# A list scheduler whose order comes from one rule, and then from three tables of offsets, leads and margins

## The chip, the cores and the metric

The kernel runs on one NeuronCore of a Trainium2 chip. The metric is the device time of one execution in microseconds (us), lower is better. Engines: PE (TensorE), DVE (VectorE), ACT (ScalarE), POOL (GpSimd) and SP (SyncE, which here issues nearly all DMAs).

## The reference: what is computed

Sliding-window attention, then a 2-D Fourier mixing, a layer norm, and a two-layer feed-forward network, all with residuals:

```python
# q, k, v: (8, 8, 576, 64); window 64
scores = np.where(mask, scale * q @ k.T, -1e9); attn = softmax(scores)
x = (attn @ v)                                   # -> (8, 576, 512)
u = x + np.real(np.fft.fft(np.fft.fft(x, axis=1), axis=2))
un = (u - mean) / sqrt(var + 1e-6)
out = u + np.maximum(un @ w_ch1, 0) @ w_ch2      # w_ch1 (512, 2048), w_ch2 (2048, 512)
```

The weights arrive as 64-bit floats, q, k and v as 32-bit floats.

## The kernel before

The 4608 rows are 36 tiles T of 128 rows (9 tiles for each pair of batches) and 18 chunks c of 256 rows for the feed-forward part. Five families of steps are declared and handed to one list scheduler:

- `attn_tile(T)`: loads kn, qn, v (L433), brings keys and queries into place (tiles below 13, the "whole" ones, by PE transposes pk, pq; the later, "split" ones as pairs of 16-bit halves, by DMA transposes, L493, L505), scores psc (L574, L581), masked maximum (L593, DVE), exponential (L601, ACT), the transposed probabilities pt (PE transpose pp, or halves `p_hi`, `p_lo` in the buffer flex and DMA transposes L632), the product pa (L663), its scaling xu (L670, L673, L682 or L680), a first radix-4 step y (L704) and its transpose py (by PE, L769 and L773, or by halves yp, L409 or L411 and L781, and a DMA transpose, L788).
- `fft(b)`, one for each batch: folds and radix steps on DVE and POOL (L815 to L850), halves fs and hs (L869), PE stages pg (L901) and pz (L933), and the results md, sent to DRAM (L961).
- `norm_tile(T)`: a gather mt from DRAM (L1011), the statistics and un (L1023 to L1039), its halves up (`u_hi` L409 or L413, `u_lo` L1058) and a DMA transpose into uhl (L1063); the first chunk uses PE transposes pu (L1051).
- `weight_piece`, `weight_scale`, `weight_split`: 32 loads of 512 KB (L1103; tiles wd or flex), three DVE conversions each (L1112, L1117, L1124), squares on ACT (L1130), a scale from the sum of squares (few L1167, the PE product pw L1148, L1151 and on), halves (L409 and L1177).
- `ffn(c)`: 16 steps f; ph (12 matmuls of 256 columns, L1220), relu hh on ACT (L1235) and its lower half on DVE (L1238), po (6 matmuls of 512 columns, L1201).

`Plan.order` simulates the five engines and picks, again and again, the step that can start first. Ties and small differences go by `prio` (`base` plus a constant written at each call); a step that may run on either of two engines takes the other one if that is sooner by more than `margin`. Buffers are rings of few slots (`RINGS`): kq 2, up 1, pt 2, big 4, ps 4 banks; for most rings the slots are handed out in the order of `prio`. Each engine then executes its list strictly as it was emitted, so an instruction that waits holds back all behind it on its engine. The ring up has one slot: the halves of a normed tile (`up`) or of a radix-4 result (`yp`) may be written only after the DMA transpose of the tile before them has landed.

In the start phase, where the planner finds PE idle for over 0.8 us, the kernel inserts small dummy matmuls (warm, L1300; called fillers here).

Of the kernel before, what the change touches and what calls it, by code (L numbers as in the profile page):

```python
# [127 lines left out]


class Op:  # L130
    __slots__ = ("eng", "dur", "lat", "fn", "deps", "outs", "prio", "wait", "ready", "allocs", "bufs", "idx", "durs", "margin", "port", "slack", "wary")


class Plan:
# [13 lines left out]
    def __init__(self, rings, fifo):  # L148
        self.rings, self.fifo, self.ops, self.gaps = dict(rings), fifo, [], []
        self.slack = self.wary = 0.0  # L150

    def op(self, eng, dur, prio, fn, reads=(), writes=(), lat=0.0, alt=(), holds=(), port=True):

        o = Op()
        o.durs = {e: d + self.FIXED[e] for e, d in ([(eng, dur), alt[:2]] if alt else [(eng, dur)])}
        o.port, o.slack, o.wary = port, self.slack, self.wary
        o.margin = alt[2] if len(alt) > 2 else self.MARGIN
        o.eng, o.dur, o.lat, o.fn, o.prio = eng, dur, lat, fn, prio  # L160
        o.idx, o.outs, o.allocs = len(self.ops), [], []
        deps = set()
        for b in reads:
            deps.update(b.writers)
        for b in writes:
            deps.update(b.writers)
            deps.update(b.readers)
            if b.ring and not b.writers and b not in o.allocs:
                o.allocs.append(b)
# [132 lines left out]
def attn_fft_ffn_kernel(ctx: ExitStack, tc: tile.TileContext, q, k, v, w1, w2, gidx, dft_d, dft_s, mask, out):  # L302
# [14 lines left out]
    plan = Plan(RINGS, ("kq", "pr", "pt", "xu", "y", "yT", "tail", "xe", "r3", "fh", "g", "mp", "f1", "f2", "hh"))  # L317
# [99 lines left out]
    def attn_tile(T, base):  # L417
# [145 lines left out]
        for jj in range(2):  # L563
# [42 lines left out]
            if whole:  # L606

                def flip_p(jj=jj):
# [7 lines left out]
                   alt=("DVE", 0.6), port=False)  # L616
# [93 lines left out]
        for bb in range(2):  # L710
# [3 lines left out]
            b = b0 + bb  # L714
# [284 lines left out]
    def norm_tile(T, base):  # L999
# [88 lines left out]
    def weight_piece(x, g, order):  # L1088
# [243 lines left out]
```

## Time and profile before

| | us |
|---|---|
| median of 3 runs | 1012.32 (1011.74 to 1016.52) |
| span of the profiled execution, first to last instruction | 1008.1 |
| median less span | 4.2 |
| PE busy | 973.4 (97%) |
| PE weight load busy | 694.3 (69%) |
| DVE busy | 682.6 (68%) |
| ACT busy | 445.8 (44%) |
| POOL busy | 155.1 (15%) |

The profiled execution's own total is not given apart from its span; what lies around the span is taken as the 4.2 us to the median. A matmul's record includes its fill, so PE counts as busy for a little of the time in which it waits; the distance from one step's start to the next is the better measure of its pace.

### The profile page before, as it was taken

The numbers are of one execution on the slowest core, as the hardware profiler recorded it, in microseconds if no ns is written. First come the engines' busy times: TensorE is split into PE (matmuls) and PEld (weight loads), VectorE is DVE, ScalarE is ACT, GpSimd is POOL, SyncE is SP. The second block draws the span as 40 slices with busy tenths as digits, with TensorE's granted clock in tenths as the row PEclk, the third lists the DMA queues.
The fourth block names the chain that finished last, engine by engine and source line by source line (L and its number), as shares of the span: only waits on it lengthen the run. The fifth ranks groups of instructions, "written<-read, shape, count | busy, mean of one in ns | idle before, by whom it ended". The sixth has DMA issues, their size and how long they took to land.

```text
span 1008.1 us, 22813 instructions
## 1 busy us (share of the span) xinstructions
PE 973.4 (97%) x8831; PEld 694.3 (69%) x8831; DVE 682.6 (68%) x1979; ACT 445.8 (44%) x1257; POOL 155.1 (15%) x162
## 2 busy tenths in 40 slices
PE   8897999999999999989999999999999999999998
PEld 6886767766676667666676666666676667666664
DVE  4699998788696779776787558776786645442121
ACT  6788756653554345443444445433443223121111
POOL 1000102011212221231023322031011100200000
PEclk9999999999999999999999999999999999999999
DMA  9999875334975796778767865968554311230000
GB/s 208 224 230 228 215 185 150 74 64 94 159 157 124 147 157 116 146 148 142 143 118 167 156 123 87 180 142 152 100 111 100 84 33 45 53 74 22 1 21 21
DMA packets 310955, 123.60 MB, mean 123 GB/s; under 512 B 292728, under 2 KB 292856, under 8 KB 310848
## 3 DMA queue, kind: packets, MB, share of 16 engines
q1 hardware_dynamic: 308128, 113.24, 56.2%
q0 software_dynamic: 2720, 8.92, 3.3%
q8 instruction: 69, 1.13, 0.5%
q14 instruction: 38, 0.31, 0.1%
HBM read 54.97 MB, written 14.17 MB: 69 GB/s over the span
## 4 chain that ended last, share of the span: by engine, by line
PE 70%; DVE 10%; DMA 10%; SPq 3%; issue 3%; ACT 2%; POOL 1%; DVEq 0%; ACTq 0%; POOLq 0%
PE ph L1220 30%; PE po L1201 28%; PE pa L663 3%; DMA uhl<-up 2%; PE pz L933 2%; DMA mt<-md,gix 2%; PE psc L581 2%; PE psc L574 1%; PE pg L901 1%; DVE y L704 1%; SPq L632 1%; DMA wd<-in_moe_w_ch 1%; DVE hh L1238 1%; PE py L769 1%; DMA flex<-in_moe_w_ch 1%
## 5 line engine op out<-in xcount | busy, mean ns | idle before, releaser
L1220 PE MATMUL ph<-uhl,w0s 128*128 128x256 f16 (+1 forms) x3384 | 425.1, 276 | 12.1 <-DVE hh L1238 11.4
L1201 PE MATMUL po<-w1s,hh 128*128 128x512 f16 (+1 forms) x1696 | 425.9, 387 | 0.0
L1220 PEld LDWEIGHTS <-w0s 128*128 128x128 f16 x3264 | 317.4, 98 | 98.1 <-issue 16.1
L1235 ACT ACTIVATE hh<-ph 128x256 f16<-128x256 f32 x272 | 104.3, 383 | 397.7 <-PE ph L1220 283.7
L1238 DVE SCALAR_TENSOR_TENSOR hh<-ph,hh 128x256 f16<-128x256 f32 x272 | 114.6, 422 | 228.0 <-ACT hh L1235 207.7
L1201 PEld LDWEIGHTS <-hh 128*128 128x128 f16 x1632 | 156.3, 98 | 137.6
L601 ACT ACTIVATE pr<-pr,nm 128x128 f32<-128x128 f32 x288 | 90.8, 402 | 5.6 <-DVE nm L593 5.6
L593 DVE CUSTOM_DVE_ANT_0 pr<-psc,mskb 128x128 f32<-128x128 f32 x288 | 65.1, 285 | 16.0 <-PE psc L574 10.5
L680 ACT ACTIVATE xu<-pa,rc 128x64 f32<-128x64 f32 x248 | 54.9, 326 | 28.0 <-DVE rc L670 11.3
L1011 POOL DMA_INDIRECT mt<-md,gix x34 | 36.1, 1061 | 135.1 <-DMA md<-mp 129.8
L1035 POOL TENSOR_TENSOR rs<-mv,mhalf 128x1 f32<-128x1 f32 x36 | 20.8, 578 | 231.5 <-DVE mv L1031 224.7
L626 POOL TENSOR_TENSOR flex<-pr,flex 128x512 f16<-128x512 f32 x22 | 28.6, 1305 | 105.5 <-ACT flex L409 57.1
L663 PE MATMUL pa<-va,pt 128*64 128x65 f16 (+1 forms) x760 | 39.0, 204 | 1.6 <-DMA pt<-flex 1.2
L663 PE MATMUL pa<-ve,pt 128*64 128x65 f16 (+1 forms) x760 | 40.3, 205 | 0.0
L933 PE MATMUL pz<-g,ds__76 97*96 97x257 f16 (+3 forms) x240 | 29.7, 273 | 2.0 <-DVE g L911 2.0
L933 PEld LDWEIGHTS <-ds__76 97*96 97x96 f16 (+1 forms) x240 | 26.7, 124 | 4.2 <-issue 3.0
L501 POOL TENSOR_TENSOR flex<-qn,flex 128x1024 f16<-128x1024 f32 x11 | 23.7, 2159 | 37.5 <-ACT flex L409 28.7
L574 PE MATMUL psc<-kst,qbd 128*128 128x128 f32 x208 | 27.4, 281 | 1.6 <-ACT qbd L409 1.6
L663 PEld LDWEIGHTS <-pt 128*64 128x64 f16 x1104 | 20.0, 111 | 11.7 <-issue 9.9
L581 PEld LDWEIGHTS <-qbd 128*64 128x64 f16 x736 | 21.6, 110 | 8.4 <-issue 7.5
L704 DVE TENSOR_TENSOR y<-xu 128x256 f32<-128x256 f32 x64 | 25.6, 442 | 2.5 <-ACT xu L680 2.4
L574 PEld LDWEIGHTS psc<-kst,qbd 128*128 128x128 f32 x208 | 24.8, 192 | 3.5 <-issue 1.6
(160 smaller groups left out, 1120.9 us busy)
## 6 DMA issues: line engine op xcount, KB each, us to landing
wd<-in_moe_w_ch SPq DMA_DIRECT2D x20, 512.0 KB
out<-xu SPq DMA_DIRECT2D x36, 256.0 KB
ve<-va SPq DMA_DIRECT2D x67, 130.0 KB
kn<-in_k SPq DMA_DIRECT2D x32, 256.0 KB
qn<-in_q SPq DMA_DIRECT2D x32, 256.0 KB
flex<-in_moe_w_ch SPq DMA_DIRECT2D x12, 512.0 KB
flex<-in_v SPq DMA_DIRECT2D x20, 256.0 KB
md<-mp SPq DMA_DIRECT2D x24, 192.0 KB
```

Source lines behind the costliest of these rows:

```text
L574: nc.tensor.matmul(p_[:, hp], qw, keys(hp, jj), start=True, stop=True)
L581: nc.tensor.matmul(p_[64 * x : 64 * x + 64, hp], qbd[i][:, jj, h, 64 * z : 64 * z + 64], keys(h, jj), start=(z == 0), stop=(z == 1),)
L593: nc.vector.tensor_tensor_reduce(out=t["pr", jj][:, hp], in0=t["ps", jj][:, hp], in1=mskb[:, m : m + P], scale=-0.125, scalar=3.0e38, op0= ...
L601: nc.scalar.activation(pr, pr, AF.Exp, bias=t["nm", jj][:, hp : hp + 1], scale=-1.0)
L663: nc.tensor.matmul(pa[64 * jj : 64 * jj + 64, hh], pt[:, sl], v_, start=(x == 0), stop=(x == len(mm) - 1))
L680: nc.scalar.mul(xv[:, hh], pa[:, hh, 0:64], rc[:, hh])
L933: nc.tensor.matmul(pz[:M, c0:c1], ds_[:NJ, a, c[0] : c[0] + c[1]], t["g", gi][:, b_, c0:c1], start=(x == 0), stop=(x == len(mm) - 1),)
L1011: nc.gpsimd.indirect_dma_start(out=mts[T], out_offset=None, in_=mds[pb][0 : HR if n < 4 else 2 * HR], in_offset=bass.IndirectOffsetOnAxis( ...
L1201: nc.tensor.matmul(t["po"][i], l_, r_, start=(f == 0 and x == 0), stop=(f == NKF - 1 and x == len(mm) - 1))
L1220: nc.tensor.matmul(ph, l_, r_, start=(x == 0), stop=(x == len(mm) - 1))
L1235: nc.scalar.activation(t["hh", f][:, 0], ph, AF.Relu)
L1238: nc.vector.scalar_tensor_tensor(out=hh[:, 1], in0=ph, scalar=0.0, in1=hh[:, 0], op0=ALU.max, op1=ALU.subtract)
```

## The change

Nothing of the computation changes, nor the number of steps. Three tables come in, looked up by the kind of the group a step belongs to (`plan.begin(kind, at)`, called at the head of each attention tile, fft, norm tile, weight piece, scale and split) and by its place k in the group or by the group's number `at`. `NUDGE[kind][k]` and `LEAD[kind][at]` are added to the step's `prio`; `BIAS[kind][k]` is added to the margin of steps with two engines (20 keeps the first engine, -20 takes the other).

```diff
+NUDGE = {
...
+    "whole": (
+        -5.3, -1, 3.7, 0, 14.6, -3.5, 1.7, 3.6, -8.3, 1, 0.1, 0, 0, -1.4, 0.2, 1.9,
...
+LEAD = {
...
+    "whole": (
+        -54.4, -12, 0.6, 0, 0.5, -15.9, -4.6, -0.6, -4.3, 0, 9.1, 1.8, 0, -0.5, 0, -3.4,
...
+BIAS = {
...
+    "split": {16: 20, 19: 0.4, 23: -0.8, 26: -0.4, 29: -1.5, 31: 0.8, 33: -0.8, 34: 0.4, 35: 1.5, 36: -0.4, 37: 0.8},
...
+    def begin(self, kind, at):
+        self.kind, self.at, self.k = kind, at, 0
 
     def op(self, eng, dur, prio, fn, reads=(), writes=(), lat=0.0, alt=(), holds=(), port=True):
...
+        shift, lead = NUDGE.get(self.kind, ()), LEAD.get({"split": "whole", "odd": "even"}.get(self.kind, self.kind), ())
+        prio += (shift[self.k] if self.k < len(shift) else 0.0) + (lead[self.at] if self.at < len(lead) else 0.0)
...
+        bias = BIAS.get(self.kind, {}).get(self.k, 0.0)
+        self.k += 1
...
-        o.margin = alt[2] if len(alt) > 2 else self.MARGIN
+        o.margin = (alt[2] if len(alt) > 2 else self.MARGIN) + bias
...
+        plan.begin("whole" if whole else "split", T)
...
+        plan.begin("even" if bb == 0 else "odd", b)
...
+        plan.begin("norm", T)
...
+        plan.begin("piece", order)
...
+        plan.begin("scale", x)
...
+        plan.begin("part", W_ORDER.index((x, g)))
...
+        plan.begin("ffn", c)
```

The program has the same matmuls but for the fillers, 87 before and 81 now. DVE has 17 instructions fewer and ACT 22 more: the upper half of yp, which DVE made for ten of the 17 tiles that have one, is now always made by ACT. In the three places below, lines of the changed kernel count about 80 higher than those of the kernel before (L1103 is now L1183).

SP's queue in the start phase, from the loads of tile 4 on (ds is the second Fourier table, flex the weight pieces that are converted next). Before:

```order
L374 DMA ds__76<-in_dft_s 128x1924
L554 DMA ve0_83<-va1_82 64x520
L433 DMA va0_81<-in_v 64x8x64 x2
L1103 DMA flex_79<-in_moe_w_ch2 128x1024
L433 DMA kn5_569<-in_k 128x8x64
L546 DMA ve0_83<-va0_81 64x520
L433 DMA qn5_593<-in_q 128x8x64
L1103 DMA flex_79<-in_moe_w_ch2 128x1024
```

And now:

```order
L633 DMA ve0_83<-va1_82 64x520
L512 DMA va0_81<-in_v 64x8x64 x2
L1183 DMA flex_79<-in_moe_w_ch2 128x1024
L512 DMA kn5_564<-in_k 128x8x64
L625 DMA ve0_83<-va0_81 64x520
L452 DMA ds__76<-in_dft_s 128x1924
L1183 DMA flex_79<-in_moe_w_ch2 128x1024
L633 DMA ve1_84<-va0_81 64x520
L512 DMA qn5_647<-in_q 128x8x64
```

The table ds stands behind the first weight piece now, and qn5 behind the second one. Further down the same queue, kn8 stood behind va1 and now stands ahead of it.

DVE's queue at the scale of the first weight matrix (few0 is its sum of squares, the three w1s rows convert one weight piece, L593 and L672 are the masked maximum of tile 10). Before:

```order
L911 SCALAR_TENSOR_TENSOR g1_1_2001<-pg1_1_2000,g1_1_2001 97x512
L1112 TENSOR_SCALAR w1s_86<-wd1_12_1996 128x512
L1117 SCALAR_TENSOR_TENSOR w1s_86<-wd1_12_1996,w1s_86 128x512
L1124 SCALAR_TENSOR_TENSOR w1s_86<-wd1_12_1996,w1s_86 128x512
L1167 TENSOR_REDUCE few0_92<-ssq1_87 128x1
L593 ISA pr10_1_1763,nm10_1_2079<-psc10_1_1764,mskb_72 128x128
L593 ISA nm10_1_2079 128x1
```

And now:

```order
L672 ISA pr10_1_1845,nm10_1_2038<-psc10_1_1846,mskb_72 128x128
L672 ISA nm10_1_2038 128x1
L948 TENSOR_TENSOR hs0_1_2007<-h0_1_1916,hs0_1_2007 128x388
L1249 TENSOR_REDUCE few0_92<-ssq1_87 128x1
L1192 TENSOR_SCALAR w1s_86<-wd1_12_1990 128x512
L1197 SCALAR_TENSOR_TENSOR w1s_86<-wd1_12_1990,w1s_86 128x512
L1204 SCALAR_TENSOR_TENSOR w1s_86<-wd1_12_1990,w1s_86 128x512
L1232 TENSOR_SCALAR few0_92<-pw0_2062 128x1
L990 SCALAR_TENSOR_TENSOR g1_1_2013<-pg1_1_2012,g1_1_2013 97x512
```

The sum of squares and the masked maximum went ahead of the conversion, and g1_1 went behind it.

ACT's queue in chunk 4, around two users of the ring up (up11 and yp16; hh rows mark the steps of the feed-forward part). Before:

```order
L409 CAST up11_4633<-un11_4630 128x512
L1235 ACTIVATE hh4_4_4661<-ph4_4_4617 128x256
L534 ACTIVATE va0_81<-flex_79 128x8x64
L680 ACTIVATE xu16_4635<-pa16_0_4636,rc16_0_4674 128x64 x4
L680 ACTIVATE xu16_4635<-pa16_1_4540,rc16_1_4614 128x64 x4
L1235 ACTIVATE hh4_5_4712<-ph4_4_4617 128x256
L409 ACTIVATE yp16_4735<-y16_4714 128x512
L1235 ACTIVATE hh4_6_4744<-ph4_6_4719 128x256
```

And now (up11 is made on DVE, behind hh4_3):

```order
L1319 ACTIVATE hh4_4_4720<-ph4_4_4698 128x256
L759 ACTIVATE xu16_4653<-pa16_0_4654,rc16_0_4717 128x64 x4
L487 CAST up12_4747<-un12_4732 128x512
L1319 ACTIVATE hh4_5_4768<-ph4_4_4698 128x256
L759 ACTIVATE xu16_4653<-pa16_1_4608,rc16_1_4724 128x64 x4
L680 ACTIVATE pr18_1_4750<-pr18_1_4750,nm18_1_4783 128x128 x4
L1319 ACTIVATE hh4_6_4820<-ph4_6_4788 128x256
L1319 ACTIVATE hh4_7_4843<-ph4_6_4788 128x256
L487 ACTIVATE yp16_4846<-y16_4801 128x512
L1319 ACTIVATE hh4_8_4871<-ph4_8_4849 128x256
```

The tile up12 moved between up11 and yp16: one hh stands between up11 and its successor where there were two, and three between that one and yp16.

## Rows read from the trace of the kernel before

**Rows 1.** The page: busy us, share of the span, instructions.

```profile
PE 973.4 (97%) x8831; PEld 694.3 (69%) x8831; DVE 682.6 (68%) x1979; ACT 445.8 (44%) x1257; POOL 155.1 (15%) x162
```

**Rows 2.** Windows by stage: busy us (x instructions) of five engines, PE clock, DMA share, GB/s.

```profile
0.00:100.00 100.00, 86.64 (x895) 76.12 (x897) 74.48 (x286) 77.04 (x232) 8.56 (x20) 0.97 0.98 222
100.00:250.00 150.00, 148.66 (x1057) 106.71 (x1054) 132.23 (x348) 87.32 (x219) 22.52 (x25) 1.00 0.53 130
250.00:700.00 450.00, 434.26 (x4358) 302.77 (x4357) 330.00 (x956) 202.07 (x580) 100.24 (x90) 1.00 0.78 143
700.00:1009.00 309.00, 303.88 (x2531) 208.67 (x2529) 145.91 (x391) 79.36 (x228) 23.81 (x27) 1.00 0.26 56
```

**Rows 3.** Chain that ended last: start, us, what; the pace of three steps.

```profile
165.18 1.73 PE ph L1220 x8
...
360.37 1.31 PE ph L1220 x12
362.56 1.40 PE po L1201 x6
```

**Rows 4.** Who waited for whom: us in total, times, longest.

```profile
PE ph L1220 <- DVE hh L1238: 11.4, 11, 2.0
...
ACT yp L409 <- DMA uhl<-up: 7.7, 3, 3.9
```

**Rows 5.** Chain, 36 to 100 us: the three loads in it.

```profile
40.70 7.67 DMA flex<-in_moe_w_ch
...
62.05 5.72 DMA kn<-in_k
...
85.23 7.60 DMA qn<-in_q
```

**Rows 6.** DVE's timeline, 36 to 62 us: conversions, idle time before each.

```profile
41.65 0.43 DVE L1112 TENSOR_SCALAR w1s<-flex 128x512 int32<-128x512 int32 x1 [3.17 <-DMA flex<-in_moe_w_ch]
...
48.40 0.43 DVE L1112 TENSOR_SCALAR w1s<-flex 128x512 int32<-128x512 int32 x1 [2.21 <-DMA flex<-in_moe_w_ch]
```

**Rows 7.** DMA issues by line: sizes of the loads that changed places.

```profile
qn<-in_q SPq DMA_DIRECT2D x32, 256.0 KB
ds__76<-in_dft_s SPq DMA_DIRECT2D x1, 481.0 KB
```

**Rows 8.** Windows in the start phase, columns as in Rows 2.

```profile
35.00:40.00 5.00, 5.00 (x65) 4.57 (x64) 2.42 (x4) 3.86 (x10) 0.00 (x0) 1.00 1.12 236
45.00:50.00 5.00, 5.00 (x33) 5.00 (x32) 2.73 (x5) 3.27 (x11) 0.00 (x0) 0.66 1.01 179
60.00:85.00 25.00, 22.41 (x277) 20.05 (x273) 23.66 (x87) 22.39 (x68) 0.72 (x2) 1.00 0.84 218
90.00:100.00 10.00, 6.89 (x58) 6.13 (x60) 9.65 (x35) 8.04 (x25) 1.75 (x2) 0.83 0.96 233
```

**Rows 9.** PE's timeline, 84 to 98 us.

```profile
85.42 3.78 PE L1300 MATMUL warm<-ident 128*128 128x256 f16 x33
92.96 0.95 PE L470 MATMUL pq<-ident,qn 128*128 128x128 f32 x4 [3.77 <-DMA qn<-in_q]
```

**Rows 10.** Timeline around pw0: PE, then DVE.

```profile
156.04 0.35 PE L1148 MATMUL pw<-few,unit 128*128 128x1 f32 x2 [1.34 <-DVE nm L593]
...
151.36 2.15 DVE L1112 TENSOR_SCALAR w1s<-wd 128x512 int32<-128x512 int32 x1
```

**Rows 11.** Timeline around yp16 (ACT, PE) and around up14 (DVE, PE).

```profile
342.05 0.63 ACT L409 ACTIVATE yp<-y 128x512 f16<-128x512 f32 x1 [3.85 <-DMA uhl<-up]
...
343.46 1.47 PE L1220 MATMUL ph<-uhl,w0s 128*128 128x256 f16 x12 [1.88 <-DVE hh L1238]
...
426.86 3.97 DVE L1058 TENSOR_TENSOR up<-un,up 128x512 f16<-128x512 f32 x1
...
431.22 1.47 PE L1220 MATMUL ph<-uhl,w0s 128*128 128x256 f16 x12 [2.02 <-DVE hh L1238]
```

**Rows 12.** Chain, 326 to 345 us: the transpose that yp16 waits for.

```profile
336.57 5.38 DMA uhl<-up
```

More of the change, by code (lines that the diff above doesn't have):

```diff
@@ L55 @@
 W_DMA, W_DMA_STEP, W_CONV, W_SQ, W_SPLIT, W_STEP = -30, 1.0, 40, 110, 60, 0.3
+NUDGE = {
+    "": (
+        5.3, 16, 0, -2.1, -7.2, -39.2, -9.3, 0, -4.4, 0.1, 13.5, 0, -7.9,
+    ),
+    "even": (
[4 rows of a table added]
+    ),
+    "norm": (
+        -1.9, -1.5, -21.3, 0, 0, -10.6, 5.7,
+    ),
+    "odd": (
[3 rows of a table added]
+    ),
+    "part": (
+        0.6, -2.9,
+    ),
+    "piece": (
+        7.7, -0.5, -5.6, -1.3, -3.1,
+    ),
+    "scale": (
+        11.5, 1.6, 1.1, 0, -2.1,
+    ),
+    "split": (
[3 rows of a table added]
+    ),
+    "whole": (
+        -5.3, -1, 3.7, 0, 14.6, -3.5, 1.7, 3.6, -8.3, 1, 0.1, 0, 0, -1.4, 0.2, 1.9,
+        0, 0.3, -1.7, 4.9, -6.6, -4.1, -0.1, 0, 1.6, 1.9, 1.2, 0.9, 2.4, -0.6, 7.5,
+    ),
+}
@@ new lines @@
+LEAD = {
+    "even": (
+        3.2, 0, 0, 0, -2.2, 8.5, -0.7, 19,
+    ),
+    "norm": (
+        -17, -1, 2.3, 7.2, 2.5, 1.5, 3.1, 10.6, 10.6, -24.5, -24.7, -9.7, 7.9, -4.6, 0.3, 4.8,
+        5.7, 19.5, -29.2, -25.5, -12, 4.3, -0.5, 10.9, 28.4, 42.9, 33.1, -11.4, 12, 53.6, 28.7, 1.4,
+        18.6, 26, 4.8, 143.5,
+    ),
+    "part": (
+        0, 6.2, -1.8, 0, -8, -53.3, -2.2, -58.3, 11.3, -43.4, -69.1, 1.9, -75.4, -63.5, -69.3, -3.6,
+        -0.7, -11.2, -77.9, -13.2, -2.1, -9.6, -5, -57.9, -0.2, -50.5, -67.2, -70.4, -63, -59.8, -138, -34.8,
+    ),
+    "piece": (
+        -17.9, 8.3, 3.8, -35.5, -5.5, 0, 0, 2.4, 0.1, -7.9, -37, 1.6, 5.9, 0.3, -2.2, 0,
+        -36, -7.6, -68.1, 1.9, -39.5, -86.2, -5.5, 4.2, -14.9, -15.7, -16.8, 4, -12.2, -7.3, -72.7, -37.6,
+    ),
+    "scale": (
+        -1.5, -63.1,
+    ),
+    "whole": (
+        -54.4, -12, 0.6, 0, 0.5, -15.9, -4.6, -0.6, -4.3, 0, 9.1, 1.8, 0, -0.5, 0, -3.4,
+        2.6, -1.9, -5, -7.2, 0, 0.5, -1.9, 0.7, -1, -6.5, 0, -4.1, -8.5, -5.4, -2.3, 12.2,
+        32.7, 36.8, 70.5, 84.4,
+    ),
+}
@@ new lines @@
+BIAS = {
+    "even": {0: 0.8, 1: -0.4, 2: -0.8, 4: 0.4, 5: 1.5, 8: 1.5, 10: 20, 11: -0.4, 12: 0.8, 13: 20, 14: -0.8, 15: -0.8, 17: -0.8, 18: -0.4, 20: 0.4, 22: 1.5, 23: 20, 25: -0.4, 28: 1.5, 31: 0.4},
+    "odd": {0: 20, 1: 0.4, 2: -0.8, 3: 20, 5: -0.4, 6: 20, 7: 1.5, 10: 1.5, 12: -0.8, 13: -0.4, 15: -0.4, 16: 0.8, 17: 1.5, 18: -0.4, 19: 0.8, 20: -0.4, 21: 20, 23: 0.8, 26: 0.8, 29: -0.4},
+    "split": {16: 20, 19: 0.4, 23: -0.8, 26: -0.4, 29: -1.5, 31: 0.8, 33: -0.8, 34: 0.4, 35: 1.5, 36: -0.4, 37: 0.8},
+    "whole": {4: 1.5, 7: 0.4, 13: 1.5, 14: -0.8, 18: 1.5, 21: -0.8, 24: 0.8, 25: -0.8, 26: -20, 27: 0.4, 28: 0.8},
+}
@@ L130 @@
 class Op:
-    __slots__ = ("eng", "dur", "lat", "fn", "deps", "outs", "prio", "wait", "ready", "allocs", "bufs", "idx", "durs", "margin", "port", "slack", "wary")
+    __slots__ = ("eng", "dur", "lat", "fn", "deps", "outs", "prio", "wait", "ready", "allocs", "bufs", "idx", "durs", "margin", "port", "slack", "wary", "group")
 class Plan:
@@ L150, in __init__ @@
         self.slack = self.wary = 0.0
+        self.begin("", 0)
+    def begin(self, kind, at):
+        self.kind, self.at, self.k = kind, at, 0
     def op(self, eng, dur, prio, fn, reads=(), writes=(), lat=0.0, alt=(), holds=(), port=True):
         o = Op()
+        shift, lead = NUDGE.get(self.kind, ()), LEAD.get({"split": "whole", "odd": "even"}.get(self.kind, self.kind), ())
+        prio += (shift[self.k] if self.k < len(shift) else 0.0) + (lead[self.at] if self.at < len(lead) else 0.0)
+        o.group = (self.kind, self.at, self.k)
+        bias = BIAS.get(self.kind, {}).get(self.k, 0.0)
+        self.k += 1
         o.durs = {e: d + self.FIXED[e] for e, d in ([(eng, dur), alt[:2]] if alt else [(eng, dur)])}
         o.port, o.slack, o.wary = port, self.slack, self.wary
-        o.margin = alt[2] if len(alt) > 2 else self.MARGIN
+        o.margin = (alt[2] if len(alt) > 2 else self.MARGIN) + bias
         o.eng, o.dur, o.lat, o.fn, o.prio = eng, dur, lat, fn, prio
```

10 rows, old and new, of the table NUDGE are left out of this document.

## The prediction

> **What bounds the kernel now.** I read the page's first line, then windows by stage, then what PE waited for, then the chain and the timelines at the longest waits. PE is busy for 97% of the span [rows 1], and its two large steps run at a steady pace once they run: 1.31 us for the 12 matmuls of a ph and 1.40 us, wait included, for the 6 of a po [rows 3]. Nothing in the change touches a matmul, so the time can only move through what PE loses beside its work. By stage that is window less busy time [rows 2]: 13.4 us in 0 to 100, 1.3 us in 100 to 250, 15.7 us in 250 to 700, and nothing but the tail after 700 (308.1 less 303.9, the last eviction and the output's way out); 34.7 us in all, the most that any order could give back besides the fillers. Two kinds of loss matter. In the start phase the chain runs through three loads [rows 5] while the DMA engines are full. In the middle PE waits 11.4 us in 11 pieces for the lower half of hh [rows 4], because DVE or ACT stands at some other instruction.
>
> The sum is made against the span of 1008.1 us; the median of the runs shown, 1012.3 us, is 4.2 us longer, and those 4.2 us I leave as they are.
>
> **The change part by part.**
>
> *Start phase, the table ds behind the first weight piece.* DVE sits idle for 3.17 us until the first flex piece lands and for 2.21 us until the second [rows 6]; the masked maximum of tile 4 and then the folds of the first Fourier step stand behind these conversions. The load of ds, 481 KB [rows 7], was issued ahead of both. At 236 GB/s in that stretch [rows 8] it takes 2.0 us of a full DMA, so the first piece lands up to 2.0 us sooner. What is late next is the second piece: ds is still ahead of it, but qn5 (256 KB [rows 7]) no longer is, which is worth 256/236 = 1.1 us. The chain goes through the second piece [rows 5], so I take 1.1 us. qn5 then lands later; DVE's conversions and folds run from 48.4 us on [rows 6], which covers it, and if they did not, qn5 would cost the 2.2 us that the 512 KB piece takes at that rate.
>
> *Start phase, kn8 ahead of va1.* The next load in the chain is kn8, 5.72 us from issue to landing [rows 5]. One 256 KB load less ahead of it is 256/218 = 1.2 us at the rate of that stretch [rows 8], and there the DMA engines are busy for 0.84 of the time, not full, so an earlier request does get an earlier answer. The Fourier step behind it needs DVE results too, so I take 1.2 us and no more.
>
> *Start phase, what stays.* The longest stop of PE is the load qn9: 3.78 us of fillers and 3.77 us of nothing [rows 9]. The loads on SP's queue ahead of qn9 are the same set in either order, and pq9 stands ahead of pu0 on PE in both. It moves with its chain and keeps its length. The six fillers fewer count nothing: they fill time in which PE would wait. Together the start gives 2.3 us; ends 0 (DMA full, the same bytes ahead of qn9) and 4.0 (the full 2.0 and 1.2 us, and 0.8 us for steps such as pk10 that now stand between pu1 and the first ph, where PE ran at a granted clock of 0.83 [rows 8]).
>
> *The weight scale.* PE waits 1.34 us at pw0 for DVE, which converts a weight piece first (2.15 us for its first row alone) and then does tile 10's masked maximum [rows 10]. Now the maximum and the sum of squares stand ahead of that conversion, and this wait goes: 1.3 us. What is late next is g1_1, which went behind the conversion and which pz1_1 needs: two ph steps of chunk 0 stand between, 1.73 us each [rows 3], so 3.5 us. That covers a conversion with a first row of 2.15 us and two more rows only just; without any cover the term turns into a loss of the same kind, 1.3 us and a little, say 1.5. I take 1.3 us of gain, ends 1.3 and -1.5.
>
> *The ring up.* At yp16 ACT stood idle for 3.85 us until the transpose of up11 had landed, 5.38 us after its issue [rows 11, 12]; hh stood behind it, and PE lost 1.88 us [rows 11]. The planner hands the slot on sooner than the chip frees it, so each pair of users that stand close together is at risk. I counted the work of PE that the program's order puts between two users of the slot: six pairs had under 5 us of it (up11 to yp16 had 4.8), now four have; under 7 us it is 16 pairs before and 21 now. Two of the six cost PE some 2 us, the other one a DVE row of 3.97 us while POOL worked [rows 11], and four cost nothing: 0.65 us each on average, so two fewer give 1.3 us. But up11 and up12 are such a pair now (3.9 us). The ends are 3.9 us of gain (no pair pays) and 2.6 us of loss (four at 0.65 for the closer pairs of the wider count, and none saved).
>
> *DVE's and ACT's stretches.* With the trace's mean durations, I added up DVE's rows between each two hh rows and set them against PE's steps between the same two. DVE exceeded PE by over 1 us in 30 of 271 stretches before and in 24 now, ACT in 15 and in 9. A scaling by that count, 45 to 33, takes 27% off the 7.5 us that are left of PE's 11.4 us [rows 4] without the two waits of the ring: 2.0 us. Most such stretches showed no loss in the trace, so I take half, 1.0 us, ends 3.0 and -2.0. DVE's 17 instructions fewer and ACT's 22 more cost nothing by themselves: ACT is busy for 44% [rows 1].
>
> *Sum:* 2.3 + 1.3 + 1.3 + 1.0 = 5.9 us off the span, so 1002.2 us, and **1006.4 us** with the 4.2 us around it. The bounds of the terms, not all at one end, leave 1002 to 1011 for this case.
>
> **A rule weighed.** In 45 to 50 us, behind a stop of PE, the granted clock was 0.66, a mean of the two levels 1.2 and 2.4 GHz, and in 90 to 100 us 0.83 although 33 fillers ran before [rows 8, 9]. The Trainium skill, page "TensorE: Matmul & The Clock Gate", Part 1, says that the low clock is the default and that sustained activity is what releases it, which speaks against taking fillers away. The trace agrees in direction. By the row the sum stands, since as many fillers are left between pz0_0 and pq9 (42 against 40, counted in the order); by the rule alone they could be worth more than nothing, and that is the fourth rival.
>
> **The rivals.**
>
> 1. *More than the terms.* The five waits that I priced are the ones I can name; the order changed everywhere. If the other waits of 250 to 700 us, 15.7 us [rows 2], fall by as much as the named ones can (about 40%, so 6.3 us in place of the 2.3 us taken there), and the start gives its 4.0, it comes to 1000.7 us. For: the losses are chance meetings of two in-order queues. Against: a new order makes new meetings too.
>
> 2. *The start gives nothing.* The DMA engines are busy for 0.98 of the first 100 us [rows 2], and the same bytes stand ahead of qn9; then its landing stays, and with it the first ph. The two middle terms and half of the third are left: 1012.3 less 3.1 = 1009.2 us. Against: 0.84 in 60 to 85 us [rows 8].
>
> 3. *The other side: yp on ACT.* All 17 yp now go through ACT, where hh stands behind them; seven did before, and three of those held ACT for 7.7 us together [rows 4]. At 3 in 7, the ten new ones meet 4.3 such waits; if each costs PE the 1.88 us of yp16 [rows 11], that is 8.1 us, and if the closer pairs under 7 us cost their 2.6 us as well and the named middle terms are lost (the start's 2.3 us stays), it is 1012.3 + 8.1 + 2.6 - 2.3 = 1020.7 us. It passes 1017.4 from three such waits on if the pairs cost that, from four on if they cost nothing. For: a new place on an in-order queue. Against: thirteen of the 17 have over 5 us of PE's work to the transpose ahead of them in the new order.
>
> 4. *The clock.* If the stretch 90 to 100 us ran at 1.2 GHz, its 6.89 busy us at 0.83 [rows 8] would take 6.89 x 0.83 / 0.5 = 11.4 us, 4.5 us more: 1010.9 us.
>
> That the change moves nothing is out: the order differs on every engine, on SP from the fourteenth DMA on.
>
> **How the numbers follow.** Forecast case 0.45 (of which 0.30 below 1007.3), more than the terms 0.20, the start gives nothing 0.17, slower by yp on ACT 0.14, the clock 0.04. A difference of 0.5%, 5.1 us, is about what a measurement here can tell from no change; it ends at 1007.3 and 1017.4. Faster 0.30 + 0.20 = 0.50; same 0.15 + 0.17 + 0.04 = 0.36; slower 0.14. The range holds the forecast case, rivals 2 and 4, most of rival 1 and the mild part of rival 3: 999 to 1014. The likeliest case's own range is 1002 to 1011.
>
> **What would show it.** Right: DVE's idle time before the two flex conversions falls from 3.17 and 2.21 us to some 1 us each; the first ph starts 2 us or more before 97 us; pw0 waits for nothing; PE's wait for hh falls from 11.4 to about 9 us. Wrong: the idle time of 0 to 100 us stays at 13.4 us; a yp on ACT waits for a transpose more than three times; PE waits at pz1_1 for g1_1, or at pa for pt. The forecast fails altogether if PE's losses in 250 to 700 us rise above 15.7 us by more than the start gives.

## The result, and the profile after

The changed kernel took 1003.31 us (median of three runs, 1002.58 to 1004.40) against 1012.03 us of the kernel before in the same series: a ratio of 0.9913, 95% interval 0.9885 to 0.9941. That is 8.7 us less, where the prediction had 5.9. A fourth run of the changed kernel took 1166.95 us at a mean granted clock of 0.811, where the others had 0.996 to 0.998, and all comparisons here leave such slow runs out (the median with it is 1003.86 us). The profiled execution took 1003.31 us with a span of 1001.5 us, so that 1.8 us lie around a span.

The changed kernel's page, busy time of its engines, as [rows 1]:

```profile
PE 975.1 (97%) x8825; PEld 692.1 (69%) x8825; DVE 663.3 (66%) x1962; ACT 452.6 (45%) x1279; POOL 155.3 (16%) x166
```

Its windows by stage, columns as in [rows 2]:

```profile
0.00:100.00 100.00, 85.50 (x874) 74.33 (x875) 75.95 (x284) 75.47 (x224) 7.39 (x19) 1.00 0.94 228
100.00:250.00 150.00, 148.03 (x1068) 105.78 (x1067) 127.84 (x346) 92.47 (x242) 23.54 (x27) 1.00 0.52 126
250.00:700.00 450.00, 444.27 (x4454) 307.53 (x4453) 323.47 (x979) 208.96 (x601) 94.55 (x89) 1.00 0.79 145
```

Window less PE's busy time gives 14.5, 2.0 and 5.7 us, where before had 13.4, 1.3 and 15.7 [rows 2]. The tail is 4.2 us in both. So PE's waiting fell by 10.0 us in 250 to 700 us, and 1.8 us of that are given back before. PE's busy time rose by 1.7 us (975.1, before 973.4), which is how 8.3 us less waiting make the profiled spans 6.6 us shorter; the medians differ by 2 us more than the spans. What PE, and ACT at the ring up, waited for, changed kernel (us in total, times, longest):

```profile
ACT up L487 <- DMA uhl<-up: 5.7, 4, 3.4
...
ACT yp L487 <- DMA uhl<-up: 3.8, 2, 2.0
...
PE ph L1304 <- ACT hh L1319: 3.5, 3, 2.1
...
PE ph L1304 <- DVE hh L1322: 1.6, 4, 0.6
```

PE waited 5.1 us for hh, in 7 pieces; before it was 11.9 us in 12, 11.4 of them the row of [rows 4]. A yp on ACT waited for a transpose twice, for 3.8 us; before it was three times, 7.7 us [rows 4]. In 250 to 700 us three stops of PE over 0.5 us are left, where before had twelve. Besides hh, PE waited there before for these, 3.8 us in all:

```profile
PE pz L933 <- DVE g L911: 2.0, 3, 1.5
PE pa L663 <- DMA pt<-flex: 1.2, 1, 1.2
PE py L773 <- DVE y L704: 0.6, 1, 0.6
```

In the changed kernel, beside hh, one row is left there:

```profile
PE pa L742 <- DMA pt<-flex: 0.4, 1, 0.4
```

### The profile page after: what moved, and what is told of

The parts are those of the page before. It is cut to its first block, busy times and chain, and to the rows that moved or that the text cites. A ratio compares the mean times of both kernels' runs of the same rounds, so it can differ in the third digit from the quotient of the medians.

```text
span 1001.5 us, 22805 instructions
## 1 busy us (share of the span) xinstructions
PE 975.1 (97%) x8825; PEld 692.1 (69%) x8825; DVE 663.3 (66%) x1962; ACT 452.6 (45%) x1279; POOL 155.3 (16%) x166
## 4 chain that ended last, share of the span: by engine, by line
PE 85%; DMA 6%; DVE 4%; ACT 2%; issue 1%; SPq 1%; POOL 0%; DVEq 0%; ACTq 0%; POOLq 0%
PE ph L1304 36%; PE po L1285 34%; PE pz L1012 3%; PE pa L742 3%; PE pg L980 2%; PE psc L660 2%; DMA mt<-md,gix 1%; DMA kn<-in_k 1%; PE psc L653 1%; PE py L848 1%; DMA uhl<-up 1%; DMA va<-in_v 1%; PE pp L691 1%; PE py L852 1%; DVE hh L1322 1%
## 5 line engine op out<-in xcount | busy, mean ns | idle before, releaser
L680 ACT ACTIVATE pr<-pr,nm 128x128 f32<-128x128 f32 x288 | 91.1, 400 | 13.6 <-DVE nm L672 13.6
L672 DVE CUSTOM_DVE_ANT_0 pr<-psc,mskb 128x128 f32<-128x128 f32 x288 | 65.5, 285 | 15.4 <-PE psc L653 12.6
L759 ACT ACTIVATE xu<-pa,rc 128x64 f32<-128x64 f32 x260 | 58.1, 324 | 21.0 <-DVE rc L752 14.1
L705 POOL TENSOR_TENSOR flex<-pr,flex 128x512 f16<-128x512 f32 x21 | 26.2, 1251 | 147.5 <-ACT flex L487 86.9
L569 POOL TENSOR_TENSOR flex<-kn,flex 128x512 f16<-128x512 f32 x16 | 19.1, 1192 | 107.8 <-ACT flex L487 73.5
L660 PEld LDWEIGHTS <-qbd 128*64 128x64 f16 x736 | 21.9, 110 | 12.7 <-issue 11.6
L660 PE MATMUL psc<-kst,qbd 128*64 128x128 f16 x736 | 28.9, 222 | 0.0
L1304 PEld LDWEIGHTS ph<-uhl,w0s 128*128 128x128 f32 x120 | 22.1, 190 | 7.3 <-issue 2.4
```

Source lines behind the costliest of these rows:

```text
L660: nc.tensor.matmul(p_[64 * x : 64 * x + 64, hp], qbd[i][:, jj, h, 64 * z : 64 * z + 64], keys(h, jj), start=(z == 0), stop=(z == 1),)
L672: nc.vector.tensor_tensor_reduce(out=t["pr", jj][:, hp], in0=t["ps", jj][:, hp], in1=mskb[:, m : m + P], scale=-0.125, scalar=3.0e38, op0= ...
L680: nc.scalar.activation(pr, pr, AF.Exp, bias=t["nm", jj][:, hp : hp + 1], scale=-1.0)
L759: nc.scalar.mul(xv[:, hh], pa[:, hh, 0:64], rc[:, hh])
L1304: nc.tensor.matmul(ph, l_, r_, start=(x == 0), stop=(x == len(mm) - 1))
```

## Experiments

Each run stands beside runs of the kernel before on the same chip (medians there 1011.3, 1013.0 and 1014.3 us for e1 to e4, e5 to e8 and e9 to e12). "Idle" is PE's, window less busy time, from the one profiled execution of each kernel, which need not be a typical one: it took 1012.3 us in e5, 1014.8 in e7 (the slowest of twelve), 1017.8 in e10 (likewise) and 1000.2 in e12 (the fastest of six).

| kernel | median us | ratio, 95% interval | idle 0 to 250 | idle 250 to 700 | idle from 700 |
|---|---|---|---|---|---|
| before | | 1 | 14.7 | 15.7 | 4.2 |
| changed | 1003.3 | 0.9913 (0.9885 to 0.9941) | 16.5 | 5.7 | 4.2 |
| e1 start tables | 1022.1 | 1.0108 (1.0070 to 1.0146) | 18.6 | 12.5 | 11.9 |
| e2 middle tables | 1024.7 | 1.0141 (1.0107 to 1.0176) | 17.4 | 17.0 | 5.2 |
| e3 nudge hh on DVE | 1012.4 | 1.0012 (0.9980 to 1.0044) | 16.3 | 9.0 | 6.1 |
| e4 nudge po | 1030.5 | 1.0227 (1.0144 to 1.0309) | 17.8 | 16.3 | 13.6 |
| e5 before, two places up | 1009.2 | 0.9957 (0.9930 to 0.9984) | 16.1 | 11.5 | 4.3 |
| e6 changed, two places up | 1004.2 | 0.9929 (0.9903 to 0.9955) | 18.4 | 6.0 | 4.5 |
| e7 before, thin POOL | 1006.9 | 0.9931 (0.9905 to 0.9957) | 16.4 | 12.7 | 4.2 |
| e8 changed, thin POOL | 1000.0 | 0.9866 (0.9827 to 0.9905) | 16.7 | 2.5 | 4.4 |
| e9 before, loads moved | 1011.8 | 0.9969 (0.9948 to 0.9991) | 15.3 | 16.7 | 4.1 |
| e10 before, fillers | 1012.6 | 0.9984 (0.9956 to 1.0013) | 12.2 | 14.9 | 4.3 |
| e11 changed, ident first | 1003.1 | 0.9885 (0.9854 to 0.9917) | 16.5 | 6.1 | 4.2 |
| e12 e11 and fillers | 1004.9 | 0.9896 (0.9867 to 0.9925) | 14.4 | 4.9 | 4.2 |

### Is any other order as good? (e1 to e4)

e1 keeps the rows of the tables for the start phase, e2 those for the middle:

```diff
 NUDGE = {
...
-    "even": (
...
-    "norm": (
...
-    "odd": (
...
-    "split": (
...
 LEAD = {
...
-    "whole": (
...
+    'whole': (-54.4, -12, 0.6, 0, 0.5, -15.9, -4.6, -0.6, -4.3, 0, 9.1, 1.8, 0),
```

That is e1's edit; LEAD and BIAS lose the same kinds, and the leads of whole stop at tile 12. In e2 the other kinds go, and the leads of whole are zero up to tile 12.

e3 and e4 are the kernel before with one planned duration changed:

```diff
-                op("DVE", 0.33, -10, lambda g=h_part: g(1), [bph], [bh], holds=[bpair], port=False)
+                op("DVE", 0.34, -10, lambda g=h_part: g(1), [bph], [bh], holds=[bpair], port=False)
...
-            op("PE", 1.73 if plain else 1.3, 1e6 + 32 * c + 2 * max(f, 1) + 5, go, [bh, Bw[1][f + at]], bpo)
+            op("PE", 1.73 if plain else 1.31, 1e6 + 32 * c + 2 * max(f, 1) + 5, go, [bh, Bw[1][f + at]], bpo)
```

> Only the rows of the three tables for the start phase (kinds "", whole, piece, part, scale and the leads of tiles 0 to 12); the rest is zero. Theory A (the gain is the middle's own order, found by the tables row by row, and the start gives nothing): PE's loss in 250 to 700 us is again like that of the kernel before, 12 to 18 us, since the scheduler's order there falls anew; 1009 to 1014 us. Theory B (the start gives its 2 to 4 us and pw0 its 1.3): 1006 to 1009 us, the first ph before 95.5 us. Theory C (any new order of the middle gives the same 10 us): 1002 to 1006 us.

> Only the rows for the middle (kinds even, odd, norm, split and the leads of tiles 13 on). Theory A: most of the gain is here, PE's loss in 250 to 700 us 6 to 9 us against 15.7 before, 1002 to 1006 us. Theory B: the start's and pw0's gain are missing, and the middle has 13 to 16 us of loss, 1008 to 1012 us. A third reading: the tables only fit each other, and half of them is one more arbitrary order: 1008 to 1016 us, PE's loss in 250 to 700 us 12 us or more.

> The kernel before with one number of the planner changed by 0.01 us (its assumed time of the lower half of hh on DVE, 0.33 to 0.34): no table, the start phase unchanged to about 160 us, and an order in the middle that is as far from the kernel before as the changed kernel's. Theory A (the order of before is an average draw, the tables' is a chosen one): loss in 250 to 700 us 12 to 19 us, 1008 to 1016 us. Theory C (before was an unlucky draw): 5 to 10 us of loss there, 1002 to 1007 us.

> As the run before it, a second draw: the planner's assumed time of a po step 1.30 to 1.31. Theory A: loss in 250 to 700 us 12 to 19 us, 1008 to 1016 us. Theory C: 5 to 10 us of loss, 1002 to 1007 us.

Three of the four are slower than before, by 1.1 to 2.3% (e4's interval is wide, 1.4 to 3.1%: three runs from 1027.6 to 1039.8 us), beyond every expectation, and the fourth is the same within 0.4% (with 9.0 us of idle time in the middle, what theory C had, but theory A's time). The two halves of the tables cost 11 and 13 us alone and win 9 together: of the readings of e2 the third comes nearest, and it holds for e1 as well. A planned duration that is longer by 0.01 us moved the time by 2.3% in e4. So a new order is no gain by itself; of these draws the order of before was a good one already, and the tables hold a better one, as a whole. All four have a wait that neither before nor the changed kernel has: PE at the head of a chunk, for the transposes of its rows. PE's timeline in e2 at 444, in e1 at 796 and in e4 at 804 us (start, us, what, idle before and its releaser):

```profile
444.47 1.86 PE L1251 MATMUL ph<-uhl,w0s 128*128 128x256 f16 x8 [6.89 <-DMA uhl<-up]
```

```profile
796.52 0.80 PE L1251 MATMUL ph<-uhl,w0s 128*128 128x256 f16 x3 [6.92 <-DMA uhl<-up]
```

```profile
803.71 2.50 PE L1220 MATMUL ph<-uhl,w0s 128*128 128x256 f16 x11 [8.13 <-DMA uhl<-up]
```

In all, e1 to e4 waited 7.5, 11.3, 7.1 and 10.8 us for it. It is not the whole of their loss: e3 paid 7.1 us and came out even, since its other waits fell. e1, e2 and e4 paid a second time: PE's busy time rose by 4.0, 7.2 and 7.6 us over before, and in the 5 us around the end of each of the three stops above or just behind it the granted clock was 0.55 (e2, 445 to 450 us), 0.56 (e1, 795 to 800) and 0.51 (e4, 802 to 807). These transposes were issued late: in e2 at 439.97 us, when PE had stood for 2.4 us, in e1 3.5 and in e4 4.7 us after PE had stopped. In before too the issue of the last transpose for chunks 4, 6, 13 and 15 ends only 2.6 to 4.3 us ahead of the chunk's first ph, in the changed kernel 2.8 to 7.1 us: an order that issues one a few us later makes PE wait.

### The ring up (e5, e6)

From 224 us on every second of its users writes into 2 KB that the weights have left free; the planner knows nothing of it, so the order stays:

```diff
+    def up_slot(name, view):
+        users[1] += 1
+        if users[0] == 32 and users[1] % 2:
+            return view(ws[1][:, 16].bitcast(F16))
+        return view(sb([P, 2 * DM], F16, "up", name))
...
-            t["yp"] = sb([P, 2, 4, P], F16, "up", f"yp{T}")
+            t["yp"] = up_slot(f"yp{T}", lambda x: x.rearrange("p (z a e) -> p z a e", z=2, a=4))
```

(`up` in the same way; users[0] counts the weight pieces that are split.)

> The kernel before in its own order, but from 224 us on (when the last weight piece is split and its old 2 KB are free) every second user of the ring up writes into those 2 KB, so that it waits for the transpose two users back. Theory A (a third of the middle's loss is this ring): PE's stops behind yp16 at 340 us (2.05), behind a yp on DVE at 578 us (1.34) and behind a yp on ACT at 683 us (2.18) go, 5.6 us, 1005 to 1007.5 us. Theory D (the queues are so full that the next waiting instruction takes its place): 1 to 3 us of gain, 1009 to 1011 us.

> The changed kernel in its own order with the same second place. Theory A: the tables have taken the ring's waits off PE's path already, one stop of 1.14 us at 344 us is left, 1002 to 1004 us, so the gap between before and after shrinks by 4 to 5 us when both have two places. Theory E (the gain is not in this ring): the gap stays as it is.

The gain of before is 0.4% (0.2 to 0.7%), and its idle time in 250 to 700 us falls by 4.2 us; the changed kernel's does not fall (5.7 and 6.0). Theory A was right on the place and 1 to 2 us too high on the size; the time, 1009.2 us, lies where theory D had it. The yp16 of [rows 11], ACT in e5 (its 2 KB lie in the tile w1s now), and the ph behind it:

```profile
345.67 0.63 ACT L417 ACTIVATE w1s<-y 128x512 f16<-128x512 f32 x1 [2.18 <-DVE y L712]
```

```profile
347.41 0.81 PE L1231 MATMUL ph<-uhl,w0s 128*128 128x256 f16 x6 [0.53 <-DVE hh L1249]
```

ACT waits for its input alone (2.18 us, before 3.85 for the transpose), and PE's stop is 0.53 us instead of 1.88. The stop at 581 us (1.18) is gone, and that at 687 us went from 2.02 to 0.70. The other stops stayed: 2.08 us behind the row that POOL stretches, 1.51 at pz, 1.39 at pa. So 4.5 of the 10.0 us (4.2, and the 0.3 by which e6 is the other way) are the ring: the tables put its users where they meet no transpose that PE feels. That is a difference of single profiles; the times agree roughly, with a gap of 8.7 us between the kernels that is 4.9 us between e5 and e6 by the medians.

### DVE beside POOL (e7, e8)

```diff
-                eng.tensor_tensor(out=kp[:, :, 1], in0=t["kn"], in1=kp[:, :, 0], op=ALU.subtract)
+                n = 1 if eng is nc.gpsimd and T > 19 else H
+                eng.tensor_tensor(out=kp[:, 0:n, 1], in0=t["kn"][:, 0:n], in1=kp[:, 0:n, 0], op=ALU.subtract)
```

(and the same for the lower halves of qn, pr and up; the part that is cut off is left out of the computation. The one slot of the ring up lies in the weights' 2 KB from 224 us on in both, and is still one slot.)

> The kernel before in its own order; the lower halves that POOL writes (flex of kn, qn and pr from tile 20 on, up from tile 10 on) are cut to an eighth or a quarter of their columns, the rest of the halves keeps old numbers, so part of the computation is left out. Theory F (DVE's instructions stretched beside POOL cost PE 4.5 us in before: 2.19 at 427 us behind a row of 3.97 us, 1.68 at 624 us, 0.67 at 373 us): 1006 to 1008.5 us, DVE's stretched rows over 0.5 us fall from 17 to under 8. If they cost nothing by themselves: 1010 us or more.

> The changed kernel with the same cut of POOL's lower halves (part of the computation left out). Theory F: little is left to gain, since DVE's rows are stretched by 7 us there against 20 and none of PE's larger stops stands behind one: 1002.5 to 1004 us. If POOL's steps matter through the transposes behind them instead, both kernels gain alike, 3 us or more.

Both gain, before 0.7% and 3.0 us of idle time in the middle, the changed kernel 3.2 us there. So POOL's work costs PE something in either order. By the medians before gains 6.2 us and the changed kernel 3.3, and 6.9 us are left between the two, where 8.7 were: most of the gap is there without POOL's work too, and whether POOL has a part of it these runs cannot tell (by their two intervals the ratio of e8 to e7 is uncertain by some 0.5%, 5 us). The first half of theory F held for the rows (stretches of DVE over 0.5 us: 17 before, 5 in e7; 7 in the changed kernel, 1 in e8), the second half fell. The row of 3.97 us of [rows 11] in e7 (start, us, what):

```profile
432.69 0.70 DVE L1070 TENSOR_TENSOR w1s<-un,w1s 128x512 f16<-128x512 f32 x1
```

PE's stop of 2.02 us behind it, the 1.51 us at pz and most of the 1.25 us at a pa (0.3 us left) are gone in e7: three of the stops that the tables removed too. Others came in their place: a stop of 3.45 us at 450 us that before doesn't have, and 3.64 us at 690 us, where before had 2.02. PE in e7:

```profile
450.47 0.64 PE L591 MATMUL psc<-kst,qbd 128*64 128x128 f16 x16 [3.45 <-DMA qbd<-flex]
...
690.40 1.86 PE L1235 MATMUL ph<-uhl,w0s 128*128 128x256 f16 x8 [3.64 <-DVE hh L1253]
```

### The start (e9 to e12)

e9 moves three loads in the finished order of the kernel before, e11 two steps in that of the changed kernel, e10 and e12 add fillers:

```diff
+        todo = list(zip(plan.order(), plan.gaps))
+        for what, spot, behind in MOVES:
+            step = todo.pop([o.group for o, _ in todo].index(what))
+            todo.insert([o.group for o, _ in todo].index(spot) + behind, step)
+        for o, gap in todo:
+            for _ in range(FILL.get(o.group, 0)):
+                nc.tensor.matmul(warm, wide[:, 0:P], wide, start=True, stop=True)
```

In e9 ds, qn5 and the v load of tile 7 go behind ve0, ve1 and kn8:

```diff
+MOVES = (
+    (('', 0, 7), ('whole', 4, 8), 1),
+    (('whole', 5, 1), ('whole', 4, 9), 1),
+    (('whole', 7, 2), ('whole', 8, 0), 1),
+)
```

In e10 the fillers are for pk5, pk8, a py of tile 6 and pq9; in e11 the identity matrix goes ahead of the memset of qbd0, and a square (junk) behind the second copy of a pu; e12 is e11 with 10 and 18 fillers:

```diff
+FILL = {('whole', 5, 3): 16, ('whole', 8, 3): 8, ('whole', 6, 27): 5, ('whole', 9, 5): 24}
...
+MOVES = (
+    (('', 0, 0), ('', 0, 8), 0),
+    (('piece', 11, 4), ('norm', 1, 4), 1),
+)
+FILL = {('whole', 8, 3): 10, ('whole', 9, 5): 18}
```

> The kernel before in its own order, with three loads alone at other places of SP's queue, as the changed kernel has them: ds behind the first flex piece, qn5 behind the second, kn8 ahead of va1. Theory S (the prediction's first term): DVE's idle time before the two flex conversions falls from 3.17 and 2.21 us to 1 to 1.6 each, kn8 lands 1 to 1.5 us sooner, and the first ph starts 2 us sooner than in before at the same clock; 1 to 2.5 us off the time. Theory T (the loads land sooner, but qn9's own chain keeps the first ph where it is): first ph within 0.7 us of before at the same clock, time within 1 us.

> The kernel before in its own order with 53 more fillers, at the four places in the start where PE stands after its planned fillers: 16 ahead of pk5 (43.5 us), 8 ahead of pk8 (67.8), 5 ahead of a py (80.7), 24 ahead of pq9 (93). Theory G (a stop of PE of some 2 us or more costs a second time, through the clock: granted 0.66 in 45 to 50 us, 0.83 in 90 to 100, and in other executions 0.50 in 70 to 75, where the 24 matmuls of a pz took 5.35 us against 2.79): the granted clock of these stretches goes to 0.9 or more, the first ph comes at 95 to 97.5 us in every execution, 1.5 to 4 us off the median, and the executions spread less. Theory H (the clock costs nothing, since loads set the pace): no change, or up to 1 us longer from fillers that stand in the way.

> The changed kernel with two steps at other places: the identity matrix first on POOL again (the tables have put it behind two memsets, and PE's fillers with pk0 behind them begin at 2.98 us instead of 1.35), and the copy of the second pu into uhl ahead of a square on ACT that waits for DVE (PE waited 1.17 us for it). Theory S (the tables' loads gave 2 us and the later opening took them away): pk0 at 4.8 us instead of 6.8, the lead is kept, first ph at 94.5 to 95.5 us against 96.9, 1001.5 to 1002.5 us. Theory T (loads set the pace in between): pk0 at 4.8 us, but psc at 41 us and all behind it where they were, first ph 96.2 to 96.9, 1003 to 1004 us.

> The run before it with 28 more fillers (10 ahead of pk8, 18 ahead of pq9). By Theory G (clock) on top of what that run gives: no stretch of the start below 0.95 of the clock, first ph at 94.5 to 97 us in every execution, 1000.5 to 1002.5 us, with less spread; by Theory H 1003 to 1004.5 us.

**e9**: 0.3% faster (0.1 to 0.5%), by the time theory S; the first ph came at 95.95 us, 1.2 us sooner than in before's profile, between the two theories. DVE's idle time before the two conversions is what the prediction asked for:

```profile
39.01 0.43 DVE L1130 TENSOR_SCALAR w1s<-flex 128x512 int32<-128x512 int32 x1 [0.99 <-DMA flex<-in_moe_w_ch]
...
44.44 0.43 DVE L1130 TENSOR_SCALAR w1s<-flex 128x512 int32<-128x512 int32 x1 [0.88 <-DMA flex<-in_moe_w_ch]
```

**e10**: the fillers did to the clock what theory G says, and the time did not follow (interval 0.9956 to 1.0013). First e5, which has the start phase of before, then e10, in the windows 45 to 50, 70 to 75 and 95 to 100 us (last three columns: granted clock, DMA share, GB/s):

```profile
45.00:50.00 5.00, 5.00 (x33) 5.00 (x32) 3.50 (x10) 3.27 (x11) 0.00 (x0) 0.66 1.20 267
70.00:75.00 5.00, 5.00 (x25) 4.78 (x25) 1.05 (x5) 0.96 (x4) 0.00 (x0) 0.50 0.88 235
...
95.00:100.00 5.00, 2.64 (x11) 2.25 (x12) 4.83 (x27) 3.28 (x13) 1.75 (x2) 0.65 1.14 252
```

```profile
45.00:50.00 5.00, 5.00 (x51) 4.67 (x53) 4.44 (x14) 4.89 (x14) 0.00 (x0) 1.00 1.08 245
70.00:75.00 5.00, 5.00 (x64) 4.63 (x64) 4.67 (x18) 4.14 (x11) 0.00 (x0) 1.00 0.72 187
...
95.00:100.00 5.00, 4.86 (x51) 3.70 (x51) 4.79 (x9) 4.94 (x14) 0.00 (x0) 1.00 0.74 198
110.00:115.00 5.00, 5.00 (x17) 3.44 (x17) 4.83 (x18) 2.75 (x6) 0.66 (x1) 0.75 0.30 74
```

Its first ph came at 96.2 us, but then PE stood 1.49 us at a py for DVE, the clock fell at 110 us instead, and the first lower half of hh in chunk 1 was at 180.2 us (before 174.4). That profile is the slowest of its twelve executions. In the other eleven the mean granted clock was 0.995 to 0.999, where before had 0.986 to 0.996 on that chip: the fillers did hold the clock, and the time did not follow, theory H. **e11**: pk0 starts at 5.16 us instead of 6.80, and the wait for the second uhl copy is 0.24 us instead of 1.17, but the first ph came at 97.54 us (at a granted clock of 0.71 in 90 to 95 us, where the changed kernel's profile had 1.00): theory T for the opening. No gain from the earlier identity matrix shows: pk8 started at 67.53 us, 1.1 us later than in the changed kernel. The time, 1003.1 us, cannot be told from the changed kernel's, nor can that of e12 (in its profile clock 1.00 throughout and the first ph at 96.4 us, median 1004.9). Neither is shown to beat it.

## Why the prediction was right or wrong

**The forecast** (1006.4 us, faster by over 0.5% likeliest) was right in sign; the time lies in its own range of 1002 to 1011. The terms behind it were not right one by one: no gain of the start shows, and the ring's and the other waits' in the middle were too small, so that the errors partly cancel. Two of its signs of being wrong came too: the idle time of 0 to 100 us did not fall below 13.4 us (14.5), and PE waited at pa for ACT's pt, 2.0 us in four pieces (before 0.2), though less for pt's transposes by DMA (0.4, before 1.2).

**The start, 2.3 us.** The loads did in part what the working says. Ahead of the first conversion DVE was idle for 1.54 us in the changed kernel and 3.17 before [rows 6], and other profiles agree (0.42 to 2.80 with the moved load, 3.50 to 3.69 in e3, e4, e5 and e7, whose start is that of before). Ahead of the second it was 1.25 and 2.21 us, but 0.42, 0.92 and 1.16 in e5, e7 and e4, so that this wait differs as much between executions as between orders. Moved alone, the loads are worth 0.1 to 0.5% in e9. In the changed kernel the first ph started at 96.94 us, 0.2 sooner than before. The stop at pq9 moved with its chain, as the prediction says: pq9 started 1.4 us sooner (91.53, before 92.96 [rows 9]). But it did not keep its length, and by the profile it is ACT's xu that ended it, not the load:

```profile
91.53 0.66 PE L549 MATMUL pq<-ident,qn 128*128 128x128 f32 x4 [2.90 <-ACT xu L759]
```

In e3, e4, e5, e7 and e9, with the order of before (in e9 but for its three loads), it was 3.0 to 3.1 us, put down to DVE's masked maximum; of these profiles only that of before has the load at its end. The step that failed is the one behind it: the sum let the first ph move with pq9, but between the two it took 5.41 us instead of 4.19. The chain there (start, us, what):

```profile
91.94 1.18 DVE un L1118 x2
...
94.22 0.75 DVE w1s L1204
94.96 0.65 DVE w0s L1204
...
95.69 0.72 ACT junk L1210 x2
96.41 0.48 ACT uhl L487
...
96.94 2.00 PE ph L1304 x8
```

The copy of pu into uhl stood on ACT behind the square (junk) of a weight piece whose conversion DVE did late: the tables put a new wait at the head of a queue, for 1.17 us. I had priced PE's steps that come in between (pk10, 0.8 us, as an end), not ACT's. In e11, with that wait at 0.24 us, it still took 4.92 us, at the lower clock there. One profile can also mislead here, as the clock of the start differs between executions: the five kernels with the start of before (before, e3, e4, e5, e7) had the first ph at 97.2, 97.7, 97.3, 102.0 and 101.9 us, the three with that of the changed kernel (with e6 and e8) at 96.9, 100.4 and 98.7. The means are 99.2 and 98.7, and each group is wider than that difference (4.8 and 3.4 us): that the start gave anything isn't shown, and 2.3 us are not excluded.

**The weight scale, 1.3 us.** Right in mechanism: pw0 waits for nothing, and pz waits nowhere for g. The stage did not gain, since a py at 228.7 us now waits 1.25 us for DVE and a pa at 107 us 0.69 us; idle time there went from 1.3 to 2.0 us.

**The ring, 1.3 us.** Right mechanism, too small: some 4 us by e5 and e6 (4.5 by the profiles). The failing step is the price, "0.65 us each on average" for close pairs: it assumed that two of six cost PE some 2 us, one of them by POOL. Three stops were the ring's, at 343, 581 and 687 us, 5.1 us in all, and I had traced only the first to it. PE's record of the last one in the kernel before:

```profile
687.14 1.03 PE L1220 MATMUL ph<-uhl,w0s 128*128 128x256 f16 x8 [2.02 <-DVE hh L1238]
```

Its releaser is a DVE row; only one step further back, on ACT, does the transpose show. Counting pairs in the order was the weaker tool: the number of pairs under 7 us rose, from 16 to 21, and the waits fell.

**DVE's and ACT's stretches, 1.0 us.** The rest of the middle's fall is 10.0 - 4.5 = 5.5 us. The waits for hh fell by 6.8 us (11.9 to 5.1), 4.5 of them the ring's, so that 2.3 us are left for this term: the count of 45 to 33 pointed the right way, and its 2.0 us were nearer than their half. The other 3.3 us were not in the sum at all: the waits at pz, pa and py, 3.8 us before, which it put at nothing. The 5.5 us are known by place (1.51 us at a pz, 1.25 at a pa, 2.02 behind the row of 3.97 us, 1.15 at 555 us are gone, and 2.13 us at 550 us is new), not by one cause. POOL may have a part: DVE's rows that are stretched by over 0.5 us fell from 17 to 7, and three of these stops are gone in e7 as well. That it is fewer meetings of two in-order queues is argued, not shown apart from the ring.

**The 4.2 us around the span** were wrong: the time is 1.8 us longer than the span in every run on record, so the profiled execution of before was some 2 us quicker than the median of its runs. The spans differ by 6.6 us, the medians by 8.7. Part of the 2 us may be the clock: its mean was 0.996 in the profile of before, 0.986 to 0.998 in its other executions, the longest at the lower values, and 0.996 to 0.998 in the changed kernel. That it makes the gain is unlikely, since in e10 a clock of 0.995 to 0.999 brought no gain that could be told; that it has no part isn't shown.

**The rivals.** The first (more than the terms) is what the middle did, at 10 us instead of the 6.3 it gave it. The second (the start gives nothing) fits what the profiles show, but for another reason than its own: the loads landed sooner. The third (yp on ACT) did not happen. The fourth (the clock) went the other way in the profile: the changed kernel's start ran at a granted clock of 1.00 throughout, before at 0.66 and 0.83 in two places [rows 8]. It is no property of the order, since with the same start it was 0.71 in 70 to 75 us in e6 and 0.70 in 95 to 100 us in e8. A rival was missing, and e1, e2 and e4 show it: a chunk's transposes come too late, 7 to 8 us at once, in orders that are 1 to 2% slower. It was worth a chance on the slower side well above what the yp rival got, and before's trace hints at it only through the short lead of those transposes.

## What to carry to other kernels

When in-order queues are emitted by a list scheduler, 0.01 us in one planned number can move the time by 2%, so an order has to be timed as a whole, and half of a found order was worth less than nothing here. Price a ring that is handed on too early by every stop that ends behind it, followed two engines back, not by counting close pairs; a second place for it, where memory becomes free, gave about half of the gain without touching the order. Ask which waits the sum leaves out: here they gave a third of the middle's fall. And before crediting an earlier load, look at what stands ahead of the last small copy of its chain on the engine that makes it.

## What the runs showed of the hardware

- **One stop can cost twice.** In e5 PE stood 2.70 us for a load, the granted clock fell to 0.50, the lower of its two levels (1.2 and 2.4 GHz), and a pz of 24 matmuls took 5.35 us; in e10, where fillers run ahead of that load and PE stood 0.36 us, 2.79 us:

```profile
69.73 1.12 PE L478 MATMUL pk<-ident,kn 128*128 128x128 f32 x4 [2.70 <-DMA kn<-in_k]
70.64 5.35 PE L941 MATMUL pz<-g,ds__76 97*96 97x257 f16 x24
```

```profile
67.44 0.66 PE L483 MATMUL pk<-ident,kn 128*128 128x128 f32 x4 [0.36 <-DMA kn<-in_k]
67.93 2.79 PE L946 MATMUL pz<-g,ds__76 97*96 97x257 f16 x24
```

  In the profile of before the same load came sooner and the clock held. The stops of 7 to 8 us in e1, e2 and e4 were followed by a granted clock of 0.51 to 0.56. Not every stop does this: behind the 2.90 us at pq9 the changed kernel's clock stayed at 1.00. Executions of before spread from 1008.1 us at a mean granted clock of 0.998 to 1019.0 us at 0.991 on one chip; that such stops make the spread is argued, and the fillers of e10, which raised the mean clock, did not shorten the time.
- **POOL can hold DVE over two of its rows.** The 3.97 us of [rows 11] end at 430.83 us, 0.56 us after the second of two POOL rows, back to back, has ended (427.03 and 429.12 us, 2.14 and 1.15 us long); with POOL's rows cut it took 0.70 us. The Trainium skill, page "SBUF — State Buffer", section "Who interferes with whom", says that a DVE instruction with two SBUF inputs contends with a GpSimd instruction that reads SBUF, and that the port pair they share is an exclusive lock. The trace agrees, and shows the wait go on over the next one:

```profile
427.03 2.14 POOL L501 TENSOR_TENSOR flex<-qn,flex 128x1024 f16<-128x1024 f32 x1
429.12 1.15 POOL L626 TENSOR_TENSOR flex<-pr,flex 128x512 f16<-128x512 f32 x1
```

- **The same stop differs between executions.** In e9, whose order in the middle is that of before, the stop at yp16 was 1.11 us (before 1.88) and the one at 687 us 5.20 us (before 2.02), since the transpose ahead of it landed later. One stop in one profile can be off by 3 us; the sum over the stage held better, 15.7 and 16.7 us.
